# Expert steps with their own scatter buffers, six wide weight pieces instead of twelve, and half of the first matrix ahead of the transposes

## The chip, the cores and the metric

One core of a Trainium2 chip runs the whole program. The metric is the device time of one execution in microseconds; lower is better. The kernel before takes 517.69 us (median of 3 runs, 515.27 to 517.78).

The engines named below: TensorE (PE; its weight loads are PEld), VectorE (DVE), ScalarE (ACT), GpSimd (POOL) and SyncE (SP). Each runs its own queue of instructions in order and waits for the others by semaphores.

## The reference

Three parts run one after the other: a recurrent attention, a LayerNorm with a dense two-matrix block, and a block of experts. The change touches only the last, which computes for each of 1536 tokens (2 x 768, 384 features, 8 experts, 1024 hidden features):

```python
logits = np.einsum('bsd,de->bse', x, w_gate)
local_gate = 1.0 / (1.0 + np.exp(-np.einsum('bsd,de->bse', x, w_local).squeeze(-1)))
for b in range(B):
    prev_e = -1
    for s in range(S):
        fresh_e = int(np.argmax(logits[b, s]))
        if s == 0 or local_gate[b, s] < 0.5:
            e = fresh_e
        else:
            e = prev_e if prev_e >= 0 else fresh_e
        prev_e = e
        ...
        h = np.maximum(x[b, s] @ w1[e], 0.0)
        out[b, s] = p[e] * (h @ w2[e])
```

Each token goes to one expert; which one, and so how many tokens an expert has, is known only when the kernel runs.

## The kernel before

Up to about 303 us the kernel computes the attention and the dense block, sorts the tokens into one list of ids per expert, and works off the first 256 tokens of the fullest expert ahead of the rest. All that follows a hand-written order (`ORDER`) and isn't touched.

From 303 us on comes the chain of expert steps. A step takes one tile of up to 128 tokens of one expert. For every expert e there is a step t = 0 without a condition; further tiles t = 1, 2, ... stand in nested conditions (`others`, L1032), each of which every engine tests on its own, by a count that it loads into a register. An engine that finds no further tile jumps over the code of the steps left out, and raises its semaphores as if it had run them. In this data expert 2 has the tiles 0, 1 and 2, expert 4 too, experts 5 and 6 have 0 and 1, and the others have one: 14 steps.

All numbers are kept as a high and a low part whose products make up for single precision: the high part of a tensor is an ACT copy, the low part a subtraction (`split`, L143 and L148). Weights arrive as float32 in two raw sets (`raws`, loaded by SP in `load_a` and `load_b`) and are split piece by piece into two sets of high and low matrices (`fill`). A piece is 512 columns; the pieces numbered in `POOL_C` have their low part made on POOL, the others on DVE. A step t = 0 of expert e > 0 splits the six pieces of its own second matrix and the six of the next expert's first one.

A step does this, and every engine's queue has it in this order:

- `xpose_pe` (only t > 0): PE turns the tile's rows, which an indirect DMA on POOL (`gather`, L194) has fetched, into bank 7; `xpose_split` splits them into slot 1 of `xq`. For t = 0 this was done in the step t = 0 before, in slot 0.
- `turn_pe` (L970): PE turns the hidden rows `hs` of the step before into banks 2 and 3, eight transposes.
- `result` (L986, L987): the output of two steps before, in bank 4, is multiplied by its tokens' gate values `cur_p` on DVE into a buffer, and POOL scatters the rows by the ids in `cur_i` with an indirect DMA.
- `turn_split`: the turned hidden rows are split into `H`.
- `first` (L962, L963): the tile's rows times the first matrix, in two halves of 512 columns with nine products each, into banks 0 and 1, and ACT's Relu into `hs`; weight pieces stand after each half (`fl(0)`, `fl(1)`).
- t = 0 only: the rows of the next expert are turned and split, and two gathers go out (`get`).
- `second` (L982): the split hidden rows of the step before times the second matrix, 24 products into bank 4.
- the other weight pieces (`fl(2)`), and for t = 0 the loads of weights two and three experts on.
- `shift` (L947 to L951): DVE moves the ids and gate values on: next to current, and this tile's to next. The ids in `cur_i` may be overwritten only when the scatter that reads them has landed.

After the last step a tail turns, splits and multiplies what is left and scatters two results. Where a line of the profile is that of a helper (L143, L148, L194, L200), the tiles' names tell what it is.

Of the kernel before, what the change touches and what calls it, by code (L numbers as in the profile page):

```python
# [14 lines left out]
I32 = mybir.dt.int32  # L15
ACTF = mybir.ActivationFunctionType
ALU = mybir.AluOpType
# [5 lines left out]
DM = NH * HD  # L23
# [3 lines left out]
NE, EF = 8, 1024  # L27
KD = DM // 128
# [7 lines left out]
C_ID, C_MK, C_RV, C_FT, C_JT, C_IO, C_TI, C_EO, C_JH, C_NC = 0, 128, 192, 200, 204, 220, 348, 360, 361, 385  # L36
HMAX = 2 * JMAX
POOL_LO = (7, 9, 11)
POOL_C = (7, 9, 11, 2)


SEQ = [(0, 0), (0, 1), (0, 2), (0, 3), (1, 0), (0, 4), (0, 5), (1, 1), (1, 2), (1, 3), (1, 4), (1, 5)]
# [59 lines left out]
def moe_kernel(ctx: ExitStack, tc: tile.TileContext, rT, kT, rn, kn, vn, wt, un, gt, w_c, wg, w1, w2,  # L102
               cst, cst_b, out, dbg=None):
    nc = tc.nc
    PE, DVE, ACT, POOL, SP = nc.tensor, nc.vector, nc.scalar, nc.gpsimd, nc.sync
# [8 lines left out]
    B = [BB[:, i] for i in range(8)]  # L114
# [15 lines left out]
    XH = [const.tile([128, DM], F32, name=f"xh{i}") for i in range(2)]  # L130
# [5 lines left out]
    def r3(ap, n):  # L136
        return ap.rearrange("p (a b) -> p a b", a=n)
# [4 lines left out]
    def split(dst_hi, dst_lo, src, relu=False, lo_eng=None):  # L142
        ACT.activation(out=dst_hi, in_=src, func=ACTF.Relu if relu else ACTF.Copy)  # L143
        if relu:
            DVE.scalar_tensor_tensor(out=dst_lo, in0=src, scalar=0.0, in1=dst_hi.bitcast(F32),
                                     op0=ALU.max, op1=ALU.subtract)
        else:
            (lo_eng or DVE).tensor_tensor(out=dst_lo, in0=src, in1=dst_hi.bitcast(F32), op=ALU.subtract)  # L148


    raws, sets = [], []

    XR = []
# [24 lines left out]
    def fill(e, i, pool=POOL_LO):  # L178
        fill_set(raws[e % 2], sets[(e + 1) % 2], i, pool)

    def fill_set(raw, ws, i, pool=POOL_LO):
        a, c = raw
        w1h, w1l, w2h, w2l = ws
        if i < 6:
            k, n = i % 3, i // 3
            ns = slice(n * 512, n * 512 + 512)
            hi, lo, src = w1h[:, k, ns], w1l[:, k, ns], a[:, k, ns]
        else:
            n = slice((i - 6) * 512, (i - 5) * 512)
            hi, lo, src = (t.rearrange("p k f -> p (k f)")[:, n] for t in (w2h, w2l, c))  # L190
        split(hi, lo, src, lo_eng=POOL if i in pool else DVE)

    def gather(dst, off, n=NTOK):
        POOL.indirect_dma_start(dst, None, xd[0:n, :], IndirectOffsetOnAxis(ap=off, axis=0),  # L194
# [2 lines left out]
    def xpose_pe(x, i):  # L197
        px = r3(B[6 + i][:, 0:DM], KD)
        for k in range(KD):
            PE.transpose(px[:, k, :], x[:, k * 128:(k + 1) * 128], ident)  # L200
# [5 lines left out]
    if True:  # L206
# [551 lines left out]

        now = []

        def load_early():
            ast.close()
            rst = ctx.enter_context(tc.tile_pool(name="cr", bufs=1, side="right", reuse_waits="tile"))
            raws.append(raw_set(rst, 0))
            sets.append(split_set(rst, 0))
            hs_.append(rst.tile([128, EF], F32, name="hs"))
            XE[0] = rst.tile([128, 2, DM], F32, name="xe0")
            load_top()
# [133 lines left out]
        def close():  # L902
            bst.close()
            cl = ctx.enter_context(tc.tile_pool(name="cl", bufs=1, reuse_waits="tile"))
            sets.append(split_set(cl, 1))
            raws.append(raw_set(cl, 1))
            XR.extend(x2)
            XP[1] = cl.tile([128, 2, DM], F32, name="xp1")
            now.extend(cl.tile([128, 2], t, name=f"now_{n}") for n, t in (("i", I32), ("p", F32)))

        def zX(i):
            POOL.memset((XE[0], XP[1])[i], 0.0)

        def rows(e, t):

            return XP[e % 2][:, t % 2] if t else XE[e % 2][:, 0]

        def get(e, t):
            if e < NE and t < JMAX:
                gather(rows(e, t), ids[:, e, t:t + 1])  # L920
# [13 lines left out]
        with tc.manual_schedule():  # L934
            for t in ORDER.split():
                name, *a = t.split(".")
                name, _, e = name.partition(":")
# [5 lines left out]
        hs = hs_[0]  # L943
# [6 lines left out]
                DVE.tensor_copy(out=nxt_i, in_=ids[:, e, t:t + 1])  # L950
                DVE.tensor_copy(out=nxt_p, in_=tab[:, e, 1, t:t + 1])  # L951

        def first(e, i, fl):

            w1h, w1l = sets[(e + 1) % 2][:2]
            xh, xl = XT[0]
            t = slice(128 * i, 128 * i + 128)
            for n in range(2):
                ns = slice(n * 512, n * 512 + 512)
                todo = [(a_, w_, k) for k in range(KD) for a_, w_ in ((xh, w1h), (xh, w1l))] + [(xl, w1h, k) for k in range(KD)]  # L960
                for q, (a_, w_, k) in enumerate(todo):
                    PE.matmul(out=B[n], lhsT=a_[:, k, t], rhs=w_[:, k, ns], start=(q == 0), stop=(q == 8))  # L962
                ACT.activation(out=hs[:, ns], in_=B[n], func=ACTF.Relu)  # L963
                fl(n)

        def turn_pe(n):
            pt = r3(B[2 + n], 4)
# [14 lines left out]
                        PE.matmul(out=B[4][:, 0:DM], lhsT=a_[:, k, 0:128], rhs=w_[:, k, :], start=(q == 0), stop=(q == 23))  # L982
                        q += 1

        def result(o):
            DVE.tensor_scalar(out=o, in0=B[4][:, 0:DM], scalar1=cur_p, scalar2=None, op0=ALU.mult)  # L986
            POOL.indirect_dma_start(out[:, :], IndirectOffsetOnAxis(ap=cur_i, axis=0), o[:, :], None,  # L987
                                    bounds_check=NTOK - 1, oob_is_err=False)

        def step(e, t, before, o):  # L990

            if t:
                xpose_pe(rows(e, t), 1)
            if before is not None:
                for n in range(2):
                    turn_pe(n)
                result(o)
            if t:
                xpose_split(1)
                get(e, t + 1)  # L1000
            if before is not None:
                for n in range(2):
                    turn_split(n)

            todo = [] if t or e == 0 else [(e, q) for q in range(6, 12)] + [(e + 1, q) for q in range(6) if e + 1 < NE]
            parts = todo[:2], todo[2:5], todo[5:]

            def fl(n):
                for q in parts[n]:
                    fill(*q, POOL_C)  # L1010

            first(e, int(t > 0), fl)
            if t == 0 and e + 1 < NE:
                xpose_pe(rows(e + 1, 0), 0)
                xpose_split(0)
                get(e + 2, 0)
                get(e + 1, 1)
            if before is not None:

                if t + 1 < JMAX:  # L1020
                    tc.mark_branch_hint_location(f"end{e}.{t + 1}", nts[e] > 2 * t + 2, engines=[PE.engine])
                second(before)
            fl(2)
            if t == 0:
                load_a(e + 3)
                if e:
                    load_b(e + 2)
            shift(e, t)

        def others(e, t):  # L1030
            if t < JMAX:
                with tc.If(nts[e] > 2 * t, label=f"end{e}.{t}"):  # L1032
                    step(e, t, e, XR[t % 2])
                    others(e, t + 1)

        ctx.enter_context(tc.manual_schedule())
# [1 line left out]
        DVE.memset(now[1], 0.0)  # L1038
        ld_n(0)
        for e in range(NE):  # L1040
            step(e, 0, e - 1 if e else None, XH[e % 2])
            if e + 1 < NE:
                ld_n(e + 1)
            others(e, 1)
        for n in range(2):
            turn_pe(n)
        result(XH[0])
        for n in range(2):
            turn_split(n)
        second(NE - 1)  # L1050
        shift(None, 0)
        result(XH[1])


def layout(inputs):
# [70 lines left out]
```

## Time and profile before

| | before |
|---|---|
| median of 3 runs | 517.69 us (515.27 to 517.78) |
| the profiled execution's own time | 517.72 us |
| its span, first to last instruction | 515.9 us |
| mean granted TensorE clock | 0.934 |
| PE busy | 405.6 us (79%) |
| DVE busy | 333.3 us (65%) |
| POOL busy | 223.3 us (43%) |
| ACT busy | 184.0 us (36%) |
| DMA | 59.69 MB, 116 GB/s on the mean |

All rows come from the profiled execution. Busy is the time in which an engine carried out an instruction of its own; waits, branches and the issue of DMAs are not in it. A row of the timeline gives start and duration, engine, line, operation, what is written from what, the shape, how many instructions in a row are merged (x5), and in brackets how long the engine stood idle before and who released it. "DVEq" or "PEq" as a releaser is that engine's sequencer, here the raising of semaphores behind a skipped step. [...]

### The profile page before, as it was taken

Reading aid. Unit: us, or ns where it says so; the run is one execution under the profiler, and the core shown is the slowest. Engines: PE = TensorE matmul, PEld = TensorE weight load, DVE = VectorE, ACT = ScalarE, POOL = GpSimd, SP = SyncE. Lnnn points to the kernel's source line nnn. Section 1 sums busy time; section 2 is a strip of 40 time slices with the busy share of each in tenths; the row PEclk is TensorE's granted clock in tenths of the full one; section 3 lists DMA queues with packets and bytes.
Section 4 is the critical chain, followed back from the end, with each engine's and each line's share of the span. In section 5 each row is a group of like instructions: output and inputs, shape, how many; then the busy total and the mean of one; then the engine's idle time right before and its main releaser. Section 6 shows DMA issues by size and latency. Waiting matters only on the chain. (4 is left out here: it accounts for less than half of the span.)

```text
span 515.9 us, 8879 instructions
## 1 busy us (share of the span) xinstructions
PE 405.6 (79%) x3297; PEld 366.9 (71%) x3297; DVE 333.3 (65%) x685; ACT 184.0 (36%) x471; POOL 223.3 (43%) x212
## 2 busy tenths in 40 slices
PE   2447586999899799999999793596891979879675
PEld 2336575998799799889988673485881767768564
DVE  7998999758647857775785981736244543736341
ACT  1463453314135122212432541653251612707040
POOL 6879879264325412713041251635133432615141
PEclk9999799999899899999999996878996889989897
DMA  8863371051033050003309556075306270310000
GB/s 256 281 199 138 119 269 34 21 186 32 2 104 104 15 159 3 32 1 143 136 0 339 213 175 269 23 258 177 122 18 214 85 248 32 98 66 15 9 20 15
DMA packets 24848, 59.69 MB, mean 116 GB/s; under 512 B 3994, under 2 KB 10598, under 8 KB 24512
## 3 DMA queue, kind: packets, MB, share of 16 engines
q1 hardware_dynamic: 21856, 50.85, 29.0%
q0 software_dynamic: 2912, 7.88, 4.3%
q8 instruction: 38, 0.62, 0.5%
q14 instruction: 42, 0.34, 0.2%
HBM read 56.35 MB, written 5.70 MB: 120 GB/s over the span
## 5 line engine op out<-in xcount | busy, mean ns | idle before, releaser
L506 PE MATMUL banks<-wh,H 128*128 128x384 f32 x288 | 84.9, 356 | 7.6 <-DVE H L494 6.5
L962 PE MATMUL banks<-w1h,xq 128*128 128x512 f32 x168 | 64.6, 456 | 18.8 <-DVE xq L148 14.3
L148 POOL TENSOR_TENSOR w2l<-wb,w2h 128x512 fp32r<-128x512 f32 x27 | 35.0, 1304 | 63.2 <-ACT w2h L143 63.1
L506 PEld LDWEIGHTS banks<-wh,H 128*128 128x128 f32 x288 | 54.7, 196 | 9.8 <-DVE H L494 7.5
L962 PEld LDWEIGHTS banks<-w1h,xq 128*128 128x128 f32 x168 | 36.7, 221 | 30.0 <-DVE xq L148 16.0
L491 ACT ACTIVATE H<-banks 128x512 fp32r<-128x512 f32 x36 | 21.3, 594 | 80.3 <-PE banks L487 73.6
L506 PE MATMUL banks<-wl,H 128*128 128x384 f32 x144 | 49.9, 347 | 0.0
L982 PE MATMUL banks<-w2h,H 128*128 128x384 f32 x224 | 47.1, 343 | 0.0
L148 DVE TENSOR_TENSOR w1l<-wa,w1h 128x512 fp32r<-128x512 f32 x48 | 46.7, 1028 | 0.1
L487 PE MATMUL banks<-xq,wh 128*128 128x256 f32 x216 | 43.8, 301 | 0.4 <-DVE xq L470 0.4
L148 DVE TENSOR_TENSOR w2l<-wb,w2h 128x512 fp32r<-128x512 f32 x27 | 23.4, 868 | 30.4 <-ACT w2h L143 30.4
L970 PE MATMUL banks<-cs,hs 128*128 128x128 f32 x112 | 18.2, 317 | 29.1 <-DVEq L1032 21.0
L982 PEld LDWEIGHTS banks<-w2h,H 128*128 128x128 f32 x224 | 39.8, 192 | 1.0 <-ACT H L143 0.3
L963 ACT ACTIVATE hs<-banks 128x512 f32<-128x512 f32 x28 | 16.8, 598 | 58.5 <-PE banks L962 58.5
L970 PEld LDWEIGHTS banks<-cs,hs 128*128 128x128 f32 x112 | 15.1, 164 | 31.5 <-issue 31.5
L962 PE MATMUL banks<-w1l,xq 128*128 128x512 f32 x84 | 37.1, 441 | 0.0
L487 PEld LDWEIGHTS banks<-xq,wh 128*128 128x128 f32 x216 | 35.9, 202 | 1.1 <-DVE xq L470 0.6
L494 DVE SCALAR_TENSOR_TENSOR H<-banks,H 128x512 fp32r<-128x512 f32 x36 | 24.5, 684 | 18.7 <-ACT H L491 18.6
L987 POOL DMA_INDIRECT out<-xh,now_i x9 | 9.1, 1006 | 58.5 <-DVE xh L986 52.5
L143 ACT ACTIVATE H<-banks 128x512 fp32r<-128x512 f32 x28 | 15.6, 597 | 48.9 <-PE banks L970 48.9
L986 DVE TENSOR_SCALAR xh<-banks,now_p 128x384 f32<-128x384 f32 x9 | 5.6, 618 | 42.4 <-PEq L1032 22.1
L487 PE MATMUL banks<-xq,wl 128*128 128x256 f32 x108 | 31.9, 295 | 0.6 <-DVE wl L290 0.6
(234 smaller groups left out, 1055.2 us busy)
## 6 DMA issues: line engine op xcount, KB each, us to landing
wa<-in_w SPq DMA_DIRECT2D x16, 768.0 KB, 7.4
wb<-in_w SPq DMA_DIRECT2D x16, 768.0 KB, 10.3
wq<-in_w_c SPq DMA_DIRECT2D x12, 768.0 KB, 4.8
r<-in_rT SPq DMA_DIRECT2D x12, 256.0 KB, 3.9
k<-in_kT SPq DMA_DIRECT2D x12, 256.0 KB, 4.4
rn<-in_rn SPq DMA_DIRECT2D x12, 192.0 KB, 2.6
R<-in_vn SPq DMA_DIRECT2D x24, 96.0 KB, 2.6
kn<-in_kn SPq DMA_DIRECT2D x12, 192.0 KB, 3.9
```

What stands on the lines that cost most here:

```text
L143: ACT.activation(out=dst_hi, in_=src, func=ACTF.Relu if relu else ACTF.Copy)
L148: (lo_eng or DVE).tensor_tensor(out=dst_lo, in0=src, in1=dst_hi.bitcast(F32), op=ALU.subtract)
L487: PE.matmul(out=ph[:, i, :], lhsT=a, rhs=x_[:, k, :], start=(q == 0), stop=(q == 8))
L491: ACT.activation(out=hh[:, ring(n)], in_=r3(B[3 + n % 2], 2), func=ACTF.Relu)
L494: DVE.scalar_tensor_tensor(out=hl[:, ring(n)], in0=r3(B[3 + n % 2], 2), scalar=0.0, in1=hh[:, ring(n)].bitcast(F32), op0=ALU.max, op1=ALU. ...
L506: PE.matmul(out=bank_o(b, g), lhsT=a[:, f2, s][:, i], rhs=w_[:, 2 * p + i, DM:], start=(p + i + n == 0), stop=(p == NP - 1 and i == 1 and ...
L962: PE.matmul(out=B[n], lhsT=a_[:, k, t], rhs=w_[:, k, ns], start=(q == 0), stop=(q == 8))
L963: ACT.activation(out=hs[:, ns], in_=B[n], func=ACTF.Relu)
L970: PE.transpose(pt[:, k, :], hs[:, f * 128:(f + 1) * 128], ident)
L982: PE.matmul(out=B[4][:, 0:DM], lhsT=a_[:, k, 0:128], rhs=w_[:, k, :], start=(q == 0), stop=(q == 23))
L986: DVE.tensor_scalar(out=o, in0=B[4][:, 0:DM], scalar1=cur_p, scalar2=None, op0=ALU.mult)
L987: POOL.indirect_dma_start(out[:, :], IndirectOffsetOnAxis(ap=cur_i, axis=0), o[:, :], None, bounds_check=NTOK - 1, oob_is_err=False)
```

## The change

- The low parts of the weight pieces in the chain are all made on DVE, and a piece has 1024 columns: three for a first matrix, three for a second (`fill2`).
- In a step t = 0 the first half of the first matrix (nine products) stands on PE ahead of `turn_pe`; in the others it stands after it, as before. On ACT and DVE one piece of the second matrix comes ahead of `turn_split`, ACT's first Relu follows `turn_split` directly, then come two pieces, the second Relu, and after `second` the next expert's three pieces.
- `result` is done on ACT (a copy with the gate values as scale). The ids are first copied by DVE into one of four small tiles (`XO`), which go with the four result buffers, and the scatter reads them there.

```diff
-POOL_C = (7, 9, 11, 2)
...
+    def fill2(e, i):
+        a, c = raws[e % 2]
+        w1h, w1l, w2h, w2l = sets[(e + 1) % 2]
+        if i < 3:
+            split(w1h[:, i], w1l[:, i], a[:, i])
+        else:
+            n = slice((i - 3) * 1024, (i - 2) * 1024)
+            split(*(t.rearrange("p k f -> p (k f)")[:, n] for t in (w2h, w2l, c)))
...
+            XO.extend(zip((*XR, *XH), (cl.tile([128, 1], I32, name=f"oi{n}") for n in range(4))))
...
-        def result(o):
-            DVE.tensor_scalar(out=o, in0=B[4][:, 0:DM], scalar1=cur_p, scalar2=None, op0=ALU.mult)
-            POOL.indirect_dma_start(out[:, :], IndirectOffsetOnAxis(ap=cur_i, axis=0), o[:, :], None,
+        def result(n):
+            o, oi = XO[n]
+            DVE.tensor_copy(out=oi, in_=cur_i)
+            ACT.activation(out=o, in_=B[4][:, 0:DM], func=ACTF.Copy, scale=cur_p)
+            POOL.indirect_dma_start(out[:, :], IndirectOffsetOnAxis(ap=oi[:, 0:1], axis=0), o[:, :], None,
                                     bounds_check=NTOK - 1, oob_is_err=False)
 
         def step(e, t, before, o):
             if t:
                 xpose_pe(rows(e, t), 1)
+            else:
+                first_pe(e, 0, 0)
             if before is not None:
                 for n in range(2):
                     turn_pe(n)
...
             if t:
                 xpose_split(1)
                 get(e, t + 1)
+                first_pe(e, 1, 0)
+
+            todo = [] if t or e == 0 else [(e, q) for q in range(3, 6)] + [(e + 1, q) for q in range(3) if e + 1 < NE]
+            parts = todo[:1], todo[1:3], todo[3:]
+
+            def fl(n):
+                for q in parts[n]:
+                    fill2(*q)
+
+            fl(0)
             if before is not None:
                 for n in range(2):
                     turn_split(n)
-
-            todo = [] if t or e == 0 else [(e, q) for q in range(6, 12)] + [(e + 1, q) for q in range(6) if e + 1 < NE]
-            parts = todo[:2], todo[2:5], todo[5:]
-
-            def fl(n):
-                for q in parts[n]:
-                    fill(*q, POOL_C)
-
-            first(e, int(t > 0), fl)
+            first_act(0)
+            first_pe(e, int(t > 0), 1)
+            fl(1)
+            first_act(1)
```

`first_pe(e, i, n)` holds the nine products of half n, and `first_act(n)` the Relu of that half, both as they stood in `first`. The calls of `step` and of the tail name the buffer by its number.

## Rows read from the trace of the kernel before

**Rows 1.** The page, part 1: busy time, share of the span, instructions.
```profile
PE 405.6 (79%) x3297; PEld 366.9 (71%) x3297; DVE 333.3 (65%) x685; ACT 184.0 (36%) x471; POOL 223.3 (43%) x212
```

**Rows 2.** Windows cut at the steps: window, length, busy (instructions), granted clock, DMA.
```profile
376.50:386.40 9.90, 9.75 (x53) 8.60 (x53) 5.23 (x8) 7.16 (x14) 4.88 (x4) 1.00 0.06 24
386.40:398.00 11.60, 0.00 (x0) 0.01 (x1) 5.67 (x9) 1.74 (x4) 3.88 (x4) 0.65 0.59 174
398.00:410.40 12.40, 12.38 (x55) 11.05 (x56) 5.61 (x8) 7.25 (x14) 4.86 (x4) 0.77 0.32 131
410.40:426.40 16.00, 11.40 (x53) 9.41 (x51) 8.42 (x18) 4.30 (x9) 5.94 (x6) 0.89 0.64 220
...
446.90:463.30 16.40, 11.83 (x54) 9.68 (x52) 8.56 (x17) 4.49 (x9) 6.13 (x6) 0.90 0.28 93
...
473.30:489.90 16.60, 11.91 (x55) 9.76 (x53) 8.85 (x17) 4.60 (x9) 4.91 (x5) 0.90 0.03 7
```

**Rows 3.** Waits, 300 to 516 us: who for whom, total us, times, longest.
```profile
PE banks L970 <- DVEq L1032: 21.0, 3, 11.7
...
DVE now_i L947 <- DMA out<-x,now_i: 20.3, 4, 7.8
...
PE banks L962 <- DVE xq L148: 14.3, 4, 3.7
...
PE banks L970 <- PEq L1032: 8.2, 5, 6.0
...
PE banks L200 <- DMA x<-xd,ids: 4.7, 3, 2.7
```

**Rows 4.** Timeline of PE, ACT, DVE and POOL, step 3.0 and after.
```profile
378.91 1.10 PE L962 MATMUL banks<-w1h,xq 128*128 128x512 f32 x4
...
384.91 3.23 ACT L143 ACTIVATE w1h<-wa 128x512 fp32r<-128x512 f32 x6
...
385.92 5.84 DVE L148 TENSOR_TENSOR w1l<-wa,w1h 128x512 fp32r<-128x512 f32 x5
...
387.74 4.02 DVE L148 TENSOR_TENSOR w1l<-wa,w1h 128x512 fp32r<-128x512 f32 x2
...
388.11 1.28 POOL L148 TENSOR_TENSOR w2l<-wb,w2h 128x512 fp32r<-128x512 f32 x1
...
398.04 0.62 DVE L986 TENSOR_SCALAR xh<-banks,now_p 128x384 f32<-128x384 f32 x1 [5.97 <-DVEq L1032]
```

**Rows 5.** Timeline: the start of 2.0, and DVE's start in the tail.
```profile
336.35 1.94 PE L970 MATMUL banks<-cs,hs 128*128 128x128 f32 x8 [6.62 <-DVEq L1032]
336.39 0.62 DVE L986 TENSOR_SCALAR xh<-banks,now_p 128x384 f32<-128x384 f32 x1 [0.98 <-DVEq L1032]
...
502.60 0.62 DVE L986 TENSOR_SCALAR xh<-banks,now_p 128x384 f32<-128x384 f32 x1 [2.91 <-DVEq L1032]
```

**Rows 6.** Timeline of steps 2.1 and 2.2: rows' split, weight load, gather, PE.
```profile
350.49 0.47 ACT L143 ACTIVATE xq<-banks 128x384 fp32r<-128x384 f32 x1
...
353.11 1.70 SPq L166 DMA_DIRECT2D wa<-in_w  x2
...
357.29 1.03 POOL L194 DMA_INDIRECT x<-xd,ids  x1 [0.30 <-issue]
...
366.25 0.55 PE L200 MATMUL banks<-cs,x 128*128 128x128 f32 x3 [1.44 <-DMA x<-xd,ids]
```

**Rows 7.** Groups by line, shapes apart: count, busy us, mean ns, idle before.
```profile
L143 ACT ACTIVATE w1h<-wa 128x512 fp32r<-128x512 f32 x54 | 29.5, 624 | 0.0
...
L287 ACT ACTIVATE wh<-d 128x768 fp32r<-128x768 f32 x12 | 10.1, 841 | 0.3
...
L148 DVE TENSOR_TENSOR w1l<-wa,w1h 128x512 fp32r<-128x512 f32 x9 | 6.0, 683 | 0.1
...
L148 DVE TENSOR_TENSOR H<-banks,H 128x512 fp32r<-128x512 f32 x28 | 18.3, 685 | 8.5 <-ACT H L143 8.5
...
L148 DVE TENSOR_TENSOR xq<-banks,xq 128x384 fp32r<-128x384 f32 x13 | 7.1, 549 | 7.2 <-ACT xq L143 7.2
```

More of the change, by code (lines that the diff above doesn't have):

```diff
@@ L759, in moe_kernel @@
         now = []
+        XO = []
         def load_early():
@@ L951, in shift, with first_pe, first_act @@
                 DVE.tensor_copy(out=nxt_p, in_=tab[:, e, 1, t:t + 1])
-        def first(e, i, fl):
+        def first_pe(e, i, n):
             w1h, w1l = sets[(e + 1) % 2][:2]
             xh, xl = XT[0]
[L957 to L964, printed above, removed]
+            t, ns = slice(128 * i, 128 * i + 128), slice(n * 512, n * 512 + 512)
+            todo = [(a_, w_, k) for k in range(KD) for a_, w_ in ((xh, w1h), (xh, w1l))] + [(xl, w1h, k) for k in range(KD)]
+            for q, (a_, w_, k) in enumerate(todo):
+                PE.matmul(out=B[n], lhsT=a_[:, k, t], rhs=w_[:, k, ns], start=(q == 0), stop=(q == 8))
+        def first_act(n):
+            ACT.activation(out=hs[:, n * 512:n * 512 + 512], in_=B[n], func=ACTF.Relu)
         def turn_pe(n):
@@ L1032, in others @@
                 with tc.If(nts[e] > 2 * t, label=f"end{e}.{t}"):
-                    step(e, t, e, XR[t % 2])
+                    step(e, t, e, t % 2)
                     others(e, t + 1)
@@ L1040, in moe_kernel @@
         for e in range(NE):
-            step(e, 0, e - 1 if e else None, XH[e % 2])
+            step(e, 0, e - 1 if e else None, 2 + e % 2)
             if e + 1 < NE:
@@ L1046, in moe_kernel @@
             turn_pe(n)
-        result(XH[0])
+        result(2)
         for n in range(2):
@@ L1051, in moe_kernel @@
         shift(None, 0)
-        result(XH[1])
+        result(3)
 def layout(inputs):
```

## The prediction, made before the result was known

> **What bounds the kernel now.** I read the page's busy times first: TensorE (PE) leads with 79% of the span [rows 1], so no engine is full, and the question is what PE waits for in the stage that the change touches. That stage runs from 303 us to the end and consists of 14 steps; I name a step by expert and tile, 0.0, 1.0, 2.0, 2.1, 2.2, 3.0, 4.0, 4.1, 4.2, 5.0, 5.1, 6.0, 6.1, 7.0, and then the tail that finishes two results. The windows cut at the steps come next [rows 2]. Step 3.0 shows a step without a wait: 9.75 us of PE work in 9.9 us at full clock. The stretch after it has no PE work for 11.6 us. [...] Steps 5.1 and 6.1 last 16.4 and 16.6 us with 11.8 and 11.9 us of PE work, at clock 0.90.
>
> The list of waits says on whom [rows 3]. Three times (21.0 us) PE's transposes of the hidden rows wait for the branch of VectorE (DVE) at L1032: a branch that skips an unused step has to be reached by each engine, and DVE reaches it only after its queue of weight pieces. Four times (14.3 us) the first matrix waits for DVE's low half of the transposed rows. Three times (4.7 us) PE waits for a gather. Four times (20.3 us) DVE itself waits for a scatter to land before it may overwrite its ids. The timeline of 3.0 to 4.0 [rows 4] shows the first kind: five w1 pieces on DVE take 5.84 us, two of them 4.02 us, while the two GpSimd (POOL) pieces at 388.11 run; a piece alone is 0.683 us [rows 7]. DVE is blocked for about 2.7 us (4.02 less 1.3). It then takes 5.97 us to get over the branch, and PE has waited 11.7 us [rows 3].
>
> **The change, part by part.**
>
> *Pieces.* Per expert twelve pieces of 512 columns (four of them on POOL) become six of 1024, all high on ScalarE (ACT), all low on DVE. No row shows a 1024-column piece. ACT takes 0.624 us at 512 and 0.841 at 768 columns [rows 7], so 0.85 ns a column and 1.06 us at 1024; back to back (six in 3.23 us, 0.537 each [rows 4]) 0.97. DVE takes 0.685 at 512 and 0.549 at 384 columns, 1.06 ns a column: 0.683 + 0.544 = 1.23 us alone, 1.15 back to back. The far bound above is the blocked pair, 4.02 us for 1024 columns; nearest are the undisturbed rows, which I take, since no POOL piece is left. Three w1 pieces then cost DVE 3.5 us for 5.84: 2.3 us less before the branch. That POOL sheds pieces of 1.28 us is worth nothing by itself: no row has PE wait for one.
>
> *Order in a step t = 0.* PE does half of the first matrix (9 products at 0.234 us, from four in 1.10 with a last of 0.40 [rows 4], 2.1 us) ahead of the transposes. Its inputs come from the step before, so it need not wait for DVE's branch, only for DVE's last w1 piece. One piece of w2 goes ahead of the hidden rows' split, two between the two activations, three w1 pieces at the end. From the first product at s: transposes end at s+3.1 (eight take 1.94 us at the lower clock [rows 5], so about 1.0), the second half at 5.3, the next rows' transposes at 5.6, second matrix (the rest of 9.75 us, 4.2) at 9.8. ACT: hidden rows 2.7 to 3.8 (0.54 each, as any 512 columns back to back), first activation 4.3, two pieces 6.3, activation 6.8, rows 7.3, three pieces 10.2. DVE: its three low pieces start at 8.3 and end at s+11.8. So PE stands about 2 us, and the next t = 0 step starts at s+11.8; before, 4.0 began 21.5 us after 3.0 [rows 2].
>
> *Result on ACT.* 0.62 us leaves DVE. ACT pays 0.57 (the 0.47 of its 384-column copy [rows 6], and 0.1 that I add for the scale column; its far bound is the 0.62 of DVE). But ACT's instruction now reads the scale that DVE's shift copies, which stands behind all of DVE's pieces; and behind it on ACT stand the split of the rows (t > 0) or a w2 piece and the hidden rows (t = 0). This is a new wait. In a t = 1 step, with the last t = 0 product at 0: DVE's pieces end at +2.0, shift +2.2, result +2.8, rows' high half +3.3, PE starts +3.35, and DVE's low half (+3.9) is there before the seventh product needs it.
>
> *Own buffers of ids.* The DVE copy of L947 no longer waits for a scatter: 20.3 us of DVE's idle time, the longest 7.8 [rows 3]. I cost it at nothing: all four stand between DVE's split for a t = 1 step and the end of that step, beside PE's second half and second matrix, and in 2.1 and 4.1 beside PE's wait for the gather. Were that cover gone, the longest would cost its excess over 6.3 us (2.1 + 4.2), 1.5. Each step adds one id copy (0.14 us) on DVE.
>
> **The sum**, against the profiled execution's 517.72 us (span 515.9; median of three 517.69):
> - 1.0 to 2.0: step 1.0 starts as before, held by PE's own branch (6.0 us [rows 3]), at the lower clock, so its chain is 1.6 us longer: DVE done at about 331.7, PE starts then and not at 336.35 [rows 5]: 4.65. Before, 2.0 ran at half clock for nearly 6 us; a gap of 2 us may or may not drop the clock. I take 1.9 of the 2.7 us: 6.5.
> - 3.0 to 4.0: I keep the slow skip on DVE (5.97 us idle). PE does its half step at s+11.8, then waits to s+17.9; with the remaining 7.75 us of work and 1.3 us for the clock 4.0 ends at s+27.0, before at s+33.8 (376.6 to 410.4): 6.8.
> - 5.1 and 6.1: 3.35 + 2.1 + 2.1 + 4.2 = 11.75, with 0.35 for the clock 12.1, for 16.4 and 16.6 [rows 2]: 8.8.
> - 2.1 and 4.1, followed by t = 2: the same is gained in the step, but tile 2's gather is issued behind a weight load. Before, it was issued at 357.29, the load at 353.11, and PE started at 366.25, 13.1 us after the load and 17.4 after the second matrix [rows 6]; the second such place, 4.1, repeats this with 12.3 and 16.5. The load waits for DVE's pieces and moves by 2.3 us, and the gather with it: 2 x 2.3, less 2 x 1.2 for the clock, since the gap grows to over 3 us: 2.2.
> - The tail: DVE's pieces of 7.0 end about 1.5 us sooner, the skip of 2.91 us stays [rows 5]: 1.5. The last scatter and its landing stay.
> Together 25.8 us: 517.7 - 25.8 = 491.9.
>
> [...] A gather during a weight load took until the load was nearly done: issued at 357.29, its rows used at 366.25, 9 us [rows 6]. [...]
>
> Skipping a step cost DVE 0.98, 5.97 and 2.91 us of idle time [rows 4, 5]. [...]
>
> **The rivals.**
> - *All skips fast.* If new code lengths let DVE pass 3.0 and the tail in 1 us, 4.0 ends at s+22.3 (4.7 more) and the tail gains 2.3: 485. One skip of three was fast. Chance 0.18.
> - *All skips slow.* Then 2.0's transposes wait to 337.8 and 2.0 ends at 346.8 instead of 342.3: 496.4. [...] Chance 0.17.
> - *Gathers not held by the load.* 2.2 and 4.2 start as soon as PE is free, 2 x 2.4 sooner and without 2 x 1.2 of clock: 484.7. [...] For it: the issue moves as well as the load. Against it: 9 us from issue to use [rows 6]. Chance 0.12.
> - *The half is not ahead*, because its own waits also end at a branch (ACT's read of its bank, in a skipped step): 2.0 loses 1.1, 4.0 loses 2.1 to 3.9: 496. It is the case where the change doesn't do what it says. Against it: ACT reaches its branch before DVE. Chance 0.1.
> - *Slower: wide pieces at half rate on DVE.* If POOL's remaining descriptor work blocks a 1024-column piece as its pieces did, at 2.3 us a piece, DVE's last piece ends 5.5 us later in each of six steps, 33 us: 525. It decides from 2.0 us a piece (25.8 / 6 is 4.3 us, shared by the last five pieces). For it: the 4.02 us pair [rows 4]. Against it: the first three w1 pieces, before 387.74, took 1.82 us, 0.61 each, while POOL issued gathers. Chance 0.05.
>
> **How the numbers follow.** Forecast 491.9, its own range 488 to 496, chance 0.35; the rivals above 0.62; 0.03 for a gain that a later wait takes back wholly. The predicted time is 492. Low: fast skips or early gathers at 485, and both with a clock that never drops at 482. High: slow skips together with a half that isn't ahead, 500.5, and 3.5 us for pieces at 1.3 us: 504. Changes under 0.5% (2.6 us) can't be told from none. Faster 0.92, same 0.03, slower 0.05.
>
> **What would show it.** DVE's w1 pieces: 3 in 3.5 us, none over 1.3. A t = 0 step that starts about 12 us after another (18 after a slow skip), with first-matrix products ahead of the transposes. PE's wait in 5.1 on ACT's rows, about 2 us, none on DVE's. PE's wait for the gather in 2.2 and 4.2 grown to about 3 us. No wait of L947's copy for a scatter. I am wrong if ACT's result waits for more than DVE's shift, or if DVE's low pieces end later than 12.5 us after the step's start.

## The result and the profile after

The changed kernel takes 479.05 us (median; 477.34 to 484.9), the kernel before 516.48 in the same comparison: a ratio of 0.927, with a 95% interval of 0.9205 to 0.933. I had predicted 492.0 (482 to 504): right in sign, 13 us too high, and 3 us below the range. The profiled execution of after took 477.66 us (span 475.8), so between the two profiled executions 40.1 us went. One run of after (484.9 us) and one each of e7 and e9 below (485.54 and 492.14, the ones that were profiled) lie over 1.5% above the fastest of their kernel: they stand in the medians, not in the ratios.

The page of after, part 1 (to be read against [rows 1]):

```profile
PE 395.7 (83%) x3297; PEld 359.2 (75%) x3297; DVE 315.1 (66%) x673; ACT 186.9 (39%) x447; POOL 187.6 (39%) x185
```

PE does the same 3297 instructions in 9.9 us less busy time; that goes with the granted clock, a share of full speed, which from the start of 1.0 to the tail is 0.98 on the mean where it was 0.89. The rest, 30 us, is idle time that went. Windows of after, cut at steps 3.0, 4.0, 4.1, 5.1 and 6.1 (window, length, busy and instructions of PE, PEld, DVE, ACT and POOL, granted clock, DMA share and rate), as in [rows 2]:

```profile
362.90:373.10 10.20, 9.84 (x54) 8.61 (x54) 7.24 (x8) 8.41 (x12) 3.52 (x3) 1.00 0.21 63
373.10:383.40 10.30, 10.14 (x54) 8.62 (x55) 8.01 (x14) 7.57 (x12) 3.32 (x3) 1.00 0.70 235
383.40:396.70 13.30, 9.98 (x55) 8.60 (x53) 5.40 (x16) 4.73 (x9) 2.04 (x2) 1.00 0.87 322
416.60:429.00 12.40, 10.06 (x56) 8.65 (x53) 4.78 (x15) 3.91 (x8) 2.04 (x2) 1.00 0.27 93
438.70:451.00 12.30, 9.98 (x55) 8.60 (x53) 4.68 (x15) 3.79 (x8) 2.04 (x2) 1.00 0.04 9
```

Steps 3.0 and 4.0 now follow each other without the 11.6 us hole, and each is nearly full of PE work (9.84 us in 10.20). Steps 5.1 and 6.1 went from 16.4 and 16.6 us (by the windows) to 12.4 and 12.3, at full clock. The list of waits from 300 us on, as in [rows 3]:

```profile
POOL out L1000 <- ACT xh L999: 63.0, 8, 10.6
...
PE banks L972 <- ACT xq L142: 9.0, 4, 2.6
...
DVE oi L998 <- DVEq L1052: 8.3, 7, 3.0
...
PE banks L972 <- PEq L1052: 8.0, 5, 6.3
...
PE banks L209 <- DMA x<-xd,ids: 3.7, 3, 1.6
...
PE banks L981 <- DVEq L1052: 1.7, 1, 1.7
```

PE's wait for DVE's branch fell from 21.0 to 1.7 us, its wait for the transposed rows from 18.3 (14.3 on DVE [rows 3], 4.0 on ACT) to 9.0, all on ACT. DVE's 20.3 us behind scatters are gone but for 0.7. The wait for PE's own branch stayed (8.2, now 8.0).

The timeline of step 3.0 and the start of 4.0, as in [rows 4]:

```profile
362.93 0.50 PE L972 MATMUL banks<-w1h,xq 128*128 128x512 f32 x1 [0.44 <-PEq L1052]
...
365.13 1.04 PE L981 MATMUL banks<-cs,hs 128*128 128x128 f32 x8
...
368.38 2.36 DVE L147 TENSOR_TENSOR w2l<-wb,w2h 128x1024 fp32r<-128x1024 f32 x2 [0.64 <-ACT w2h L142]
...
371.14 3.50 DVE L147 TENSOR_TENSOR w1l<-wa,w1h 128x1024 fp32r<-128x1024 f32 x3
...
373.09 0.50 PE L972 MATMUL banks<-w1h,xq 128*128 128x512 f32 x1 [0.34 <-ACTq L1052]
...
374.69 0.50 PE L972 MATMUL banks<-w1l,xq 128*128 128x512 f32 x1 [0.16 <-DVE w1l L147]
...
375.91 0.15 DVE L998 COPY oi<-now_i 128x1 int32<-128x1 int32 x1 [0.96 <-DVEq L1052]
```

DVE's three w1 pieces take 3.50 us and end at 374.64, 11.7 us after the step began: both as predicted (3.5, s+11.8). But PE begins 4.0 at 373.09, while the second of the three still runs: the first two products need only the first piece, the next two the second, and so on. It waits for the last piece just once, 0.16 us. (The 0.34 us ahead of the first product are ACT's branch: the mechanism of the rival in which the half is not ahead is there, but too short to matter.) And DVE is over its branch 0.96 us after its shift, where it took 5.97.

Steps 2.1 and 2.2, as in [rows 6]: the load of a first matrix, tile 2's gather and its use.

```profile
341.48 1.23 SPq L165 DMA_DIRECT2D wa<-in_w  x2
...
344.56 1.03 POOL L203 DMA_INDIRECT x<-xd,ids  x1 [0.30 <-issue]
...
352.64 0.55 PE L209 MATMUL banks<-cs,x 128*128 128x128 f32 x3 [1.32 <-DMA x<-xd,ids]
```

From the gather's issue to its use are 8.1 us (9.0 before), and from the load's issue 11.2 (13.1 before). The wide pieces, shapes apart (count, busy us, mean ns, idle before), beside [rows 7]:

```profile
L142 ACT ACTIVATE w1h<-wa 128x1024 fp32r<-128x1024 f32 x18 | 17.9, 1088 | 0.0
L147 DVE TENSOR_TENSOR w1l<-wa,w1h 128x1024 fp32r<-128x1024 f32 x18 | 20.9, 1217 | 0.0
...
L999 ACT ACTIVATE x<-banks,now_p 128x384 f32<-128x384 f32 x6 | 3.5, 580 | 14.5 <-PE banks L993 7.0 <-issue 3.8 <-PE banks L981 3.7
```

The predicted 1.23, 1.06 and 0.57 us are 1.217, 1.088 and 0.580.

Where the 40.1 us are, by the starts of PE's steps in the two profiles:

| stretch | before | after | saved | predicted |
|---|---|---|---|---|
| up to the start of 1.0 | 318.5 | 316.3 | 2.2 | 0 |
| 1.0 and 2.0 | 30.2 | 22.4 | 7.8 | 6.5 |
| 3.0 and 4.0 | 33.6 | 20.4 | 13.2 | 6.8 |
| 5.1 and 6.1 | 33.9 | 24.7 | 9.3 | 8.8 |
| 2.1 and 4.1 | 34.3 | 27.3 | 7.1 | 2.2 |
| 7.0 and the tail | 25.4 | 24.8 | 0.6 | 1.5 |

The other steps are the same within 0.1 us.

### The profile page after: what moved, and what is told of

It is laid out like the page before. It is cut to its first block, busy times and chain, and to the rows that moved or that the text cites. A ratio compares the mean times of both kernels' runs of the same rounds, so it can differ in the third digit from the quotient of the medians.

```text
span 475.8 us, 8791 instructions
## 1 busy us (share of the span) xinstructions
PE 395.7 (83%) x3297; PEld 359.2 (75%) x3297; DVE 315.1 (66%) x673; ACT 186.9 (39%) x447; POOL 187.6 (39%) x185
## 5 line engine op out<-in xcount | busy, mean ns | idle before, releaser
L972 PE MATMUL banks<-w1h,xq 128*128 128x512 f32 x168 | 59.7, 417 | 18.3 <-ACT xq L142 9.0
L147 DVE TENSOR_TENSOR w2l<-wb,w2h 128x1024 fp32r<-128x1024 f32 (+1 forms) x27 | 29.3, 1108 | 45.0 <-ACT w2h L142 45.0
L500 ACT ACTIVATE H<-banks 128x512 fp32r<-128x512 f32 x36 | 21.3, 594 | 79.2 <-PE banks L496 72.5
L993 PEld LDWEIGHTS banks<-w2h,H 128*128 128x128 f32 x224 | 40.1, 192 | 1.2 <-ACT H L142 0.5
L1000 POOL DMA_INDIRECT out<-xh,oi x9 | 9.7, 1076 | 69.4 <-ACT xh L999 63.0
L147 DVE TENSOR_TENSOR w1l<-wa,w1h 128x512 fp32r<-128x512 f32 (+1 forms) x36 | 32.4, 951 | 0.1
L496 PE MATMUL banks<-xuh,wh 128*128 128x256 f32 x108 | 31.3, 290 | 0.0
L496 PE MATMUL banks<-xul,wh 128*128 128x256 f32 x108 | 30.6, 284 | 0.5 <-DVE xul L479 0.5
L496 PE MATMUL banks<-xuh,wl 128*128 128x256 f32 x108 | 30.5, 282 | 0.0
L142 ACT ACTIVATE w2h<-wb 128x1024 fp32r<-128x1024 f32 (+1 forms) x33 | 28.5, 903 | 2.5 <-DMA wb<-in_w 2.5
L373 POOL TENSOR_TENSOR cv<-R,c 64x384 f32<-64x384 f32 x19 | 18.8, 992 | 23.7 <-DVE c L368 22.0
L142 ACT ACTIVATE w1h<-wa 128x512 fp32r<-128x512 f32 (+1 forms) x36 | 28.1, 856 | 0.0
```

Source lines behind the costliest of these rows:

```text
L373: e.tensor_tensor(out=r3(cv[b][s], NH), in0=r3(R[b][g % 2][s, q, :], NH), in1=bc(c[s], [64, NH, HD]), op=ALU.mult)
L496: PE.matmul(out=ph[:, i, :], lhsT=a, rhs=x_[:, k, :], start=(q == 0), stop=(q == 8))
L500: ACT.activation(out=hh[:, ring(n)], in_=r3(B[3 + n % 2], 2), func=ACTF.Relu)
L1000: POOL.indirect_dma_start(out[:, :], IndirectOffsetOnAxis(ap=oi[:, 0:1], axis=0), o[:, :], None, bounds_check=NTOK - 1, oob_is_err=False)
```

## Experiments

Each time is the median; each ratio is to the kernel before, run on the same chip, with its 95% interval. "Chain" is the time from the start of 1.0 to PE's first transpose in the tail, in the profiled execution: 184.1 us before, 145.9 after. The kernels are called e1 to e16.

### The parts alone

The first three kernels put one part each into the kernel before. The pieces:

```diff
-            todo = [] if t or e == 0 else [(e, q) for q in range(6, 12)] + [(e + 1, q) for q in range(6) if e + 1 < NE]
-            parts = todo[:2], todo[2:5], todo[5:]
+            todo = [] if t or e == 0 else [(e, q) for q in range(3, 6)] + [(e + 1, q) for q in range(3) if e + 1 < NE]
+            parts = todo[:1], todo[1:3], todo[3:]
...
-                    fill(*q, POOL_C)
+                    fill2(*q)
```

> The kernel before with the wide pieces alone: six of 1024 columns per expert, none on GpSimd, at the places where the pieces stood. Theory: the pieces carry most of the gain, since DVE gets through its last three 2.3 us sooner in six steps and everything else waits for that: about 14 us, 503. If the skip after 3.0 also becomes fast, 5 us more, 498. Rival (the order and the ids carry it): under 5 us, over 512.

e1: 493.69 us, ratio 0.953 [0.948, 0.957], faster than both expectations. Of the three parts alone the wide pieces are the largest, and two slow skips are gone, though nothing at the branch was edited.

```diff
+            o, oi = XO[n]
-            DVE.tensor_scalar(out=o, in0=B[4][:, 0:DM], scalar1=cur_p, scalar2=None, op0=ALU.mult)
+            DVE.tensor_copy(out=oi, in_=cur_i)
+            ACT.activation(out=o, in_=B[4][:, 0:DM], func=ACTF.Copy, scale=cur_p)
```

> The kernel before with the result on ACT and own ids alone. Theory: next to nothing, 515 to 518, for DVE's pieces still end last and ACT now waits for the shift behind them. Rival: the 20.3 us in which DVE waited for scatters were on the path; then 505 to 510.

e2: 510.77 us, 0.986 [0.9805, 0.9915]: faster than the first expectation, and just outside the rival's. Its waits of PE:

```profile
PE banks L965 <- ACT xq L143: 21.8, 4, 5.6
PE banks L973 <- DVEq L1037: 13.6, 3, 6.6
```

The wait for DVE's branch fell by 7.4 us from the 21.0 of [rows 3], because both slow skips went fast (0.96 us at 4.0), and PE's wait for the rows is 21.8 us, all on ACT, where before had 18.3. So the gain is the skips' (with them alone, e4 below gains more, 0.981), and the part itself seems to cost. It is the first sign of what e10 shows.

```diff
             if t:
                 xpose_pe(rows(e, t), 1)
+            else:
+                first_pe(e, 0, 0)
```

> The kernel before with half of the first matrix ahead of the transposes alone; in the steps with t = 0 the weight pieces follow the Relu as before. Theory: 2.1 to 4 us at each of the two places where PE stood for DVE's branch (before 2.0 and 4.0), nothing elsewhere: 509 to 513. Rival: the half does not get ahead (its own waits end at the branch too): 517.

e3: 509.27 us, 0.985 [0.980, 0.990], as expected. The slow skips stayed.

### Slow skips and the place of the code

The skips that went fast in e1, e2 and after had only this in common: DVE's instruction count had changed. e4 changes nothing but that; the 64 added instructions stand in a condition that is never true, and so never run.

```diff
                     step(e, t, e, XR[t % 2])
+                    if e == 0 and t == JMAX - 1:
+                        for _ in range(64):
+                            DVE.memset(now[1][:, 1:2], 0.0)
```

> The kernel before with 64 DVE instructions added to the innermost condition of expert 0, which never runs: nothing is executed that was not before, but all DVE code behind it stands 64 instructions further on. If DVE's 5.97 us over the branch after 3.0 are a matter of where the code stands, they fall to about 1 us (or another skip becomes slow): 512 or 513. If they are a matter of the weight load that starts there, they stay: 517.

e4: 507.52 us, 0.981 [0.9765, 0.9855]: 10 us faster than before without any change in what runs, and 5 us faster than expected; 2.3 of these are the tail's skip, which went fast as well (0.56 us for 2.91). DVE's first instruction in 4.0, in e3 (DVE code at the places of before) and then in e4:

```profile
390.90 0.62 DVE L985 TENSOR_SCALAR xh<-banks,now_p 128x384 f32<-128x384 f32 x1 [6.83 <-DVEq L1038]
```
```profile
391.93 0.62 DVE L986 TENSOR_SCALAR xh<-banks,now_p 128x384 f32<-128x384 f32 x1 [0.97 <-DVEq L1032]
```

The same branch over the same skipped code takes 5.97 us [rows 4] or 6.83 or 0.97, by where the code lies.

The traces also show what goes on meanwhile. The profile keeps instruction transfers apart from other DMA (its queues q8 and q14). From 390 to 398.2 us in before, with the slow skip, it lists

```profile
q14 instruction: 1, 0.01, 0.6%
```

and from 373 to 376 us in after, with the fast skip at the same place, no transfer at all:

```profile
DMA packets 0, 0.00 MB, mean 0 GB/s; under 512 B 0, under 2 KB 0, under 8 KB 0
```

So it is throughout. In all 18 traces together, ten skips behind 3.0 or in the tail kept DVE idle for 2.8 us or more, and each has one or two such transfers in its idle time; none of the 34 fast skips (0.87 to 0.99 us) ahead of 2.0 and 4.0 has one. In before the transfer behind 3.0 starts at 396.04, 4.0 us into the idle time, while a weight load is under way; in the tail, with no load, it starts 0.9 us into it. These 3.1 us are the difference between 5.97 and 2.91. The load alone doesn't make a skip slow: in e4 it runs beside the fast one (0.22 MB of it from 390.8 to 392 us). So slow skips and transfers go together at these places; but for which engine a transfer is, the profile doesn't say, and no run took one away, so it isn't shown that DVE waits for it.

The same edit to the changed kernel, with `range(50)`, which brings the branch behind 3.0 to within one instruction of its place in the kernel before (the place where it lands was not matched):

> The changed kernel with 50 DVE instructions added to the innermost condition of expert 0, which never runs, so that the branch behind step 3.0 stands at the same place in DVE's code as in the kernel before (its instruction 1126). If the place decides, DVE needs 5 to 6 us over it again, PE waits at 4.0 and the time is 483 to 485. If the wide pieces or the earlier loads made the skip fast, it stays at 0.5 us and 479.

e5: 475.59 us, 0.922 [0.919, 0.925]. The slow skip didn't come back, so the place of the branch isn't all that counts; instead the tail's skip, 3.04 us in after, took 0.55. Which places are slow stays open. In every trace whose DVE code lies as in after (e6 to e9, e11), the skip at 3.0 was fast and the tail's took 2.96 to 3.52 us; so it belongs to the program, not to the run.

### Undoing one part of the change

The half ahead undone:

```diff
-            else:
-                first_pe(e, 0, 0)
...
-                first_pe(e, 1, 0)
...
+            first_pe(e, int(t > 0), 0)
             first_act(0)
             first_pe(e, int(t > 0), 1)
```

> The changed kernel without the half ahead: the first matrix is done whole behind the transposes, all else as changed (DVE's code is the same). Theory: at 2.0 and 4.0 PE stands until DVE's branch, about 3 us, and then has 2.1 us more to do; with a drop of the clock 1.5 more: 483 to 486. Rival: the pieces alone brought PE's wait down far enough that it costs under 2 us: 479 to 481.

e6: 477.07 us, 0.926 [0.922, 0.929]: no loss, against my expectation. 2.0 and 4.0 wait 2.60 us for DVE's branch, but 2.1 lasts 11.2 us (13.9 in after), 4.1 11.8 (13.3), 5.1 11.9 (12.3), and 2.2 starts at 352.4 (352.6): what PE gained ahead of the transposes it gave back one step later, waiting for ACT's rows and for the gather, which hang on DVE's shift and not on PE.

The half ahead kept, but with its products turned round, so that the first needs the last piece:

```diff
+            ks = range(KD)[::-1] if i == 0 else range(KD)
-            todo = [(a_, w_, k) for k in range(KD) for a_, w_ in ((xh, w1h), (xh, w1l))] + [(xl, w1h, k) for k in range(KD)]
+            todo = [(a_, w_, k) for k in ks for a_, w_ in ((xh, w1h), (xh, w1l))[::1 if i else -1]] + [(xl, w1h, k) for k in ks]
```

> The changed kernel with the products of a t = 0 step in the opposite order, so that the first one needs the last w1 piece of DVE (and not the first). My forecast had this wait in its sum. Theory: that it isn't there is worth 1 to 1.5 us at 2.0 and at 4.0: 481 to 482. Rival: DVE's branch, not the piece, sets when the transposes start, so it costs nothing: 479.

e7: 480.42 us, 0.930 [0.925, 0.935]. The starts of 2.0 and 4.0 wait 2.0 us where after waits 0.34: that is the wait that my sum had, and it comes from the order of the products. On the whole it costs too little to be told from after.

The weight loads behind 2.0 and 4.0 left out:

> The changed kernel without the weight loads that start behind steps 2.0 and 4.0 (the first matrices of experts 5 and 7 and the second ones of 4 and 6 are left out, so those experts compute with old weights). It shows what the loads cost the gathers for 2.2 and 4.2. Theory: the gather lands in about 3 us for 8, PE's waits of 1.3 and 0.7 us at 2.2 and 4.2 go: 477. Rival (8 us are the gather's own behind a scatter): no change, 479.

```diff
-            if t == 0:
+            if t == 0 and e not in (2, 4):
                 load_a(e + 3)
```

e8: 478.88 us, 0.9285 [0.926, 0.931]. The waits for the gather at 2.2 and 4.2 (1.32 and 0.72 us in after) are gone, so the gather was late because of the load; but the time stayed. Windows of 4.1, 5.1 and 6.1:

```profile
383.00:396.40 13.40, 10.79 (x51) 9.36 (x49) 4.99 (x16) 3.75 (x7) 2.05 (x2) 0.87 0.21 80
416.40:430.30 13.90, 11.57 (x56) 9.78 (x53) 4.75 (x15) 3.86 (x8) 2.05 (x2) 0.88 0.22 86
440.00:453.80 13.80, 11.52 (x54) 9.77 (x52) 4.71 (x15) 3.77 (x8) 2.05 (x2) 0.88 0.03 8
```

The clock is 0.87 to 0.88 where after's profile has 1.00, behind waits of the same 1.9 to 2.6 us; three such drops cost about 1.5 us each. After's trace is the exception here: in those of e5, e7, e8, e11 and e12, with the same waits of 1.9 us at 5.1 and 6.1, the clock fell there each time and each of the two steps took 13.8 to 14.0 us, where after's took 12.3. The drop at 4.1 came in e8 and e11 alone.

The w2 piece that goes ahead of the hidden rows' split put back behind the first Relu:

```diff
-            fl(0)
             if before is not None:
                 for n in range(2):
                     turn_split(n)
             first_act(0)
+            fl(0)
```

> The changed kernel with the first weight piece of a t = 0 step back behind the first Relu, and not ahead of the split of the hidden rows; everything else as changed, DVE's code at the same place. Theory: this order is what brought DVE's end forward; without it the chain of ACT and DVE is about 1 us longer in each of six steps, 484 or 485 (less where a gather is waited for anyway). Rival: ACT and DVE have slack there, 479.

e9: 486.32 us, 0.940 [0.936, 0.944], near the 484 to 485 expected: one piece in DVE's and ACT's idle time instead of behind it is worth 7 us.

### The result on ACT costs time

The result back on DVE, with the shared ids:

```diff
-            DVE.tensor_copy(out=oi, in_=cur_i)
-            ACT.activation(out=o, in_=B[4][:, 0:DM], func=ACTF.Copy, scale=cur_p)
-            POOL.indirect_dma_start(out[:, :], IndirectOffsetOnAxis(ap=oi[:, 0:1], axis=0), o[:, :], None,
+            DVE.tensor_scalar(out=o, in0=B[4][:, 0:DM], scalar1=cur_p, scalar2=None, op0=ALU.mult)
+            POOL.indirect_dma_start(out[:, :], IndirectOffsetOnAxis(ap=cur_i, axis=0), o[:, :], None,
```

> The changed kernel with the result on DVE and the shared ids, as before the change; pieces, order and half ahead as changed. My forecast gave the own ids nothing. Theory: the result costs DVE 0.6 us ahead of the low half of the rows in the t = 1 steps, and the scatters still land before PE needs what stands behind them: 479 to 482. Rival: now that DVE is through sooner, its wait for the scatter is on the path: over 485.

e10: 470.23 us, 0.911 [0.906, 0.916]: 8 us faster than the change as a whole, against both expectations. The timeline of the start of 5.1, first in after:

```profile
416.96 1.04 PE L981 MATMUL banks<-cs,hs 128*128 128x128 f32 x8
...
418.65 0.14 DVE L960 COPY now_p<-now_p 128x1 f32<-128x1 f32 x1
...
418.88 0.58 ACT L999 ACTIVATE x<-banks,now_p 128x384 f32<-128x384 f32 x1 [1.84 <-PE banks L981]
...
419.36 0.48 ACT L142 ACTIVATE xq<-banks 128x384 fp32r<-128x384 f32 x1
...
419.89 0.50 PE L972 MATMUL banks<-w1h,xq 128*128 128x512 f32 x1 [1.90 <-ACT xq L142]
```

and in e10:

```profile
412.35 1.04 PE L981 MATMUL banks<-cs,hs 128*128 128x128 f32 x8
...
412.55 0.49 ACT L142 ACTIVATE xq<-banks 128x384 fp32r<-128x384 f32 x1
...
413.14 0.48 PE L972 MATMUL banks<-w1h,xq 128*128 128x512 f32 x1
...
414.03 0.14 DVE L960 COPY now_p<-now_p 128x1 f32<-128x1 f32 x1
...
416.02 1.20 PE L972 MATMUL banks<-w1h,xq 128*128 128x512 f32 x4 [1.24 <-DVE xq L147]
```

In after ACT's result starts 0.09 us after DVE's copy of the scale, which stands behind all weight pieces (the wait is put down to PE's transposes, which had long begun; what came last is DVE's copy). The split of the rows stands behind it on ACT, and PE behind that. In e10 ACT splits the rows at once, PE does six products, and waits only 1.24 us for DVE's low half. Two things could be mixed into the 8 us: the ids, and the place of the code (e10's tail skip is fast). The next two take them apart. e13 is after with only the ACT line put back to DVE; e14 is e10 with 50 instructions that never run.

```diff
-            ACT.activation(out=o, in_=B[4][:, 0:DM], func=ACTF.Copy, scale=cur_p)
+            DVE.tensor_scalar(out=o, in0=B[4][:, 0:DM], scalar1=cur_p, scalar2=None, op0=ALU.mult)
```

> The changed kernel with the result scaled on VectorE again, the own buffers of ids kept. If the 8 us that the version with old result and shared ids gained came from ACT's result (it stood behind VectorE's shift of the ids and ahead of ACT's split of the token rows, so TensorE waited 2.6, 2.6, 1.9 and 1.9 us in 2.1, 4.1, 5.1 and 6.1 where the other version waits 1.2), TensorE waits 1.2 us again in the four steps and the time is 470 to 473 us. If it came from sharing the ids, the waits stay at 1.9 to 2.6 and the time is 477 to 480.

e13: 472.56 us, 0.915 [0.910, 0.920]. PE waits 1.4 us at most, 5.4 in all, for DVE's rows.

```diff
+                    if e == 0 and t == JMAX - 1:
+                        for _ in range(50):
+                            DVE.memset(now[1][:, 1:2], 0.0)
```

> The version with the old result and shared ids, its VectorE code behind expert 0 moved by 50 instructions that never run. If its gain over the changed kernel is the order of the work, the four waits stay at 1.2 us and the time at 469 to 473 us, up to 476 if a VectorE skip on the path turns slow (2.7 us and the clock after it). If most of it is the place of code, the steps 2.1, 4.1, 5.1 and 6.1 get longer again and the time is 476 to 480.

e14: 473.53 us, 0.914 [0.909, 0.919]. The waits are the 1.2 of e10 (4.9 in all). Two of DVE's skips turned slow (2.05 and 3.01 us), neither with PE waiting behind it. So ACT's result is the cost, by its waits and by the clock that fell after them in e5, e7, e8, e11 and e12 (none of the traces of e10, e13, e14 and e16, with waits of 1.2 to 1.4 us, has a drop there), and the own ids cost nothing that can be told.

The half ahead was free to lose in e6, where ACT's late result held PE anyway. Without that (e15: e10 with the diff of e6):

> The version with the old result and shared ids, without the first half ahead of the transposes: so the kernel before with wide pieces in the new order alone. If the half ahead is worth nothing because the row gathers set when 2.2 and 4.2 start, and these are issued by the time of VectorE's shift, 2.0 and 4.0 start 2.3 us later, 2.2 and 4.2 at the old time, and the time is 469 to 473 us. If it was worth nothing only under ACT's late result, it costs 2.3 us in 2.0 and 4.0 and about 0.5 to 1 in 5.1, 6.1: 474 to 477.

e15: 475.59 us, 0.921 [0.916, 0.926]. PE's waits:

```profile
PE banks L981 <- DVEq L1049: 5.2, 2, 2.6
...
PE banks L972 <- DVE xq L147: 2.8, 4, 0.7
```

It gives up 2.3 us at each of two starts and gets 0.5 back in each of four steps. The chain is 142.9 us against 139.8 in e10 and 141.9 in e14, so the half ahead is worth 1 to 3 us in the profiled executions; by the medians it is 2 to 5, though the intervals of e14 and e15 overlap.

### Three that gained nothing

e11 issues the gather of the next tile ahead of the result's scatter on POOL:

```diff
                 for n in range(2):
                     turn_pe(n)
+                if t:
+                    get(e, t + 1)
                 result(o)
             if t:
                 xpose_split(1)
-                get(e, t + 1)
```

> The changed kernel with the gather of the next tile issued ahead of the result's scatter in a t > 0 step, and so some 3 us sooner. If the gather's landing goes by its issue, PE's waits of 1.3 and 0.7 us at 2.2 and 4.2 vanish: 477. If it goes by the end of the weight load, nothing moves: 479.

e11: 480.02 us, 0.9275 [0.923, 0.932]. The gather was issued ahead of the load (338.98, the load 343.97), and 2.2 and 4.2 no longer wait; three clock drops (at 388, 422 and 446 us) took it back, as in e8.

e12 is e5 with a branch hint for PE at expert 0's skip:

```diff
+            if before is None:
+                tc.mark_branch_hint_location(f"end{e}.1", nts[e] > 2, engines=[PE.engine])
             if t == 0 and e + 1 < NE:
                 xpose_pe(rows(e + 1, 0), 0)
```

> The changed kernel with two things: the 50 never executed DVE instructions of the run before (475.6 there), and a hint to PE for the branch of expert 0, the only one that has none, where PE stood 6.2 us before step 1.0. If that stand is the fetch of the code behind the branch, a hint ahead of time takes most of it: 470 to 472. If it is DVE or ACT that PE waits for, nothing changes: 475.6.

e12: 477.17 us, 0.921 [0.915, 0.926], like e5; PE's branch behind 0.0 still takes 6.07 us.

e16 is e10 with instructions on PE that never run:

```diff
+                    if e == 0 and t == JMAX - 1:
+                        for _ in range(24):
+                            PE.transpose(r3(B[2], 4)[:, 0, :], hs[:, 0:128], ident)
```

> The version with the old result and shared ids, with 24 transposes on TensorE that never run put into the last condition of expert 0, so that TensorE's code behind expert 0 moves and VectorE's doesn't. If the 6.1 us that TensorE takes over its skip between 0.0 and 1.0 in every trace hang on the place of the code, as VectorE's skips do, it falls to under 1 us and with it the 10.2 us at half clock behind it: 458 to 464 us. If they don't hang on it, 469 to 473.

e16: 474.47 us, 0.919 [0.913, 0.924], a little above the second expectation. PE's branch still takes 5.95 us: this one moved neither by 24 instructions nor by a hint. In all 18 traces an instruction transfer of 16 KB (q8) starts 2.6 to 2.9 us before PE goes on, and none falls into PE's 29 skips of 0.52 to 0.55 us; that PE waits for it isn't shown.

## Why the prediction was wrong in size

**What held.** The price and the end of DVE's wide pieces; the half step ahead of the transposes; 5.1 and 6.1 at 12.3 us where I had 12.1, with the 2 us wait on ACT's rows (1.90 and 1.88); no wait of L947's copy for a scatter; PE's own branch unmoved. Neither sign of being wrong that I had named appeared: ACT's result waits for DVE's shift alone, and DVE's low pieces end at s+11.7. For 5.1 and 6.1 it was in part luck: in five of the other traces with these waits the clock fell and they took 13.8 to 14.0 us.

**3.0 to 4.0, 6.4 us of the miss.** The step that failed is "I keep the slow skip on DVE (5.97 us idle)". It took 0.96: 5.0 us. Nearly all of the rest is the 1.3 us of clock that I charged, an estimate of mine; 4.0 took 12.40 us at 0.77 before [rows 2] and 10.30 at 1.00 now. Starting from the first piece instead of "DVE's last w1 piece" gained PE 1.5 us at the start, but that start alone is worth little (e7). The rival of fast skips had the right mechanism here, with a chance of only 0.18. The trace of before had the slow skip twice, and the number 0.98 beside it; e4 shows that the same code in another place runs it in 0.97, and each of the ten slow skips has an instruction transfer in it, none of the 34 fast skips ahead of 2.0 and 4.0. Why one place is slow and another isn't, no run shows.

**2.1 and 4.1, 4.9 us.** The failed term is "less 2 x 1.2 for the clock", 2.4: the clock was 1.00 through 4.1. The other 2.5 is that the gather gained more than the load's 2.3 us: in 2.1 it was issued 5.8 us into the step where it was 8.6, and took 8.1 us instead of 9.0. PE's wait for it, which I had growing to about 3 us, was 1.32 and 0.72. That the load delays it held (in e8 and e11, without the load beside or ahead of it, both waits are gone).

**1.0 and 2.0, 1.3 us,** by a start of 12.2 instead of 13.2 us after 1.0 and again no drop of the clock. **The start of 1.0, 2.2 us,** can't be put down to the change: in e3 it is 314.5, in e2 319.9.

**The tail, 0.9 us too much:** its skip stayed slow, as I had it (3.04, predicted 2.91), but DVE was through its pieces only 1.1 us sooner and not 1.5, and PE's work in the tail took 7.4 us for 7.0, at half clock for part of it (5.8 in e8, with the clock at 1.00).

**The range.** Its low end took the rivals of fast skips (7.0 us) and of early gathers (7.2) one by one. By their own prices the two together give 477.7, so 482 was not the least that my own terms allowed.

**What I had not priced at all** is on the other side: "this is a new wait" was seen and put into the chain of 5.1, where it gave the right 12 us, but never set against the result left on DVE. There the step takes 11.7 us and the kernel 470 to 474. The forecast was right on 5.1 with a change that costs time there.

Like for like, in ratios, from kernels whose skips at 3.0 and in the tail are fast: the kernel before with its code moved (e4) 0.981, with wide pieces (e1) 0.953, with the pieces in the new order (e15) 0.921, with the half ahead (e10 and e14) 0.911 and 0.914, with the result on ACT and own ids (e5) 0.922, and after, whose tail skip is slow, 0.927. Each has an interval of about 0.005 either way (2.6 us), so the small ones are rough. At 517 us that is 10 us for the place of the code, 14.5 for the pieces, 16.5 for their order, 3.5 to 5 for the half ahead (1 by e16, 0.919), 4 to 5.5 lost again by the result on ACT, and 2.5 lost by the tail's skip. Of my terms, those for 3.0 and the half ahead had mixed these: I had priced the starts of 2.0 and 4.0 by the half ahead, while the earlier w2 piece and the cheaper pieces on DVE bring most of it. The version of e10 beats both kernels; e13, with own ids, lies within its interval.

## What to carry to other kernels

Where a skip costs microseconds on one engine, add instructions that never run and time it again before any number is put on the change: the place of code was worth 10 us here, twice what the half ahead brought. Then ask the profile whether an instruction transfer falls into the skip's idle time, as in all ten slow skips on DVE here. Before work is moved to an idle engine, ask what its operands wait for and what stands behind it there: ACT had time, but its result waited for a scale that DVE copies last, and held the rows' split. Small weight pieces belong into the idle time ahead of a chain, not behind its first link (7 us, e9).

## What was not expected of the hardware

- At 2.0, at 4.0 and in the tail a skip on DVE took 0.55 to 0.99 us of idle time or 2.8 to 6.8, for the same code, by the place of the code in the program (5.97 us before, 0.97 in e4); unused instructions elsewhere changed which skips were slow (e4, e5, e14). An instruction transfer fell into each of the ten slow skips.
- PE's skip behind 0.0 took 5.95 to 6.61 us in all traces, with and without a hint and with its code moved; the granted clock was half for 10.2 us in each, from within about 1 us of its start.
- Behind waits of PE of 1.9 to 2.6 us the granted clock fell in some executions (e5, e7, e8, e11, e12 at 5.1 and 6.1: about 1.5 us lost each time; 0.88 in e8) and not in others of nearly the same kernel (after: 1.00). In e8 and e11 the gather's waits of 1.32 and 0.72 us went, and the total stayed (478.88 and 480.02 us for 479.05).
- A gather took 8.1 us from issue to use beside a weight load; without the load (e8) PE used its rows 6.6 us after the issue and didn't wait for it.
